# Chunk 0's first channel product in seven block products, batch 1's v loaded whole, two small transfers taken out

## The chip, the core and the metric

The kernel runs on one core of a Trainium2 chip, in one launch. Time is in microseconds (us) of that core, and lower is better. The core has five engines that run side by side and wait for each other by semaphores: TensorE (PE in the profile, its weight loads PEld) does matmuls, VectorE (DVE), ScalarE (ACT) and GpSimd (POOL) work element by element, and SyncE (SP) issues the DMA transfers. Each engine takes its own instructions strictly in order: one that waits holds back all behind it.

## The reference

Three layers follow each other. Inputs are float32; the batch is 2, the sequence 768, the model width 512.

```python
# 1: attention, 8 heads of 64: near scores in a window of 16, far scores on block maxima of k
k_sum = k.reshape(B, H, nb, 32, D).max(axis=3)
v_sum = v.reshape(B, H, nb, 32, D).mean(axis=3)
a = softmax([scores near, scores on k_sum + log(32)])
x = a @ concat([v, v_sum])
# 2: mixer
h = relu(x^T @ w_tok1) @ w_tok2            # 768 -> 256 -> 768, over tokens
u = x + h^T
y = u + relu(u @ w_ch1) @ w_ch2            # 512 -> 1536 -> 512, over channels
# 3: second mixer, xk and xr mix a token with the one before it
k = relu(xk @ w_k); v = (k * k) @ w_v      # 512 -> 1024 -> 512
out = sigmoid(xr @ w_r) * v
```

## The kernel before

**Precision.** A float32 product is made of three matmuls (`mm3`, L189 to L192): each operand is split into a rounded part ("high") and the rest ("low"), and high·high, high·low and low·high are summed in PSUM. Splitting costs one ScalarE operation (high) and one VectorE operation (low) for each tile of 128x512. Weights come as packed words; `conv_base` (`ca`) and `conv_top` (`cn`) on ScalarE and `conv_join` (`cj`, L428 and L429) on VectorE unpack a raw tile in place, then `conv_high` (`ch`) and `conv_low` (`cl`) split it. `conv_join` has the extra instruction L428 only for a tile for which `conv_top` was not called.

**Tiling.** Attention goes by 12 query tiles, 0 to 5 of batch 0 and 6 to 11 of batch 1: `scores` (`sc`), `softmax` (`max`: a VectorE maximum over 704 columns and a subtraction), `exp_near`/`exp_far` (`en`, `ef`), transposes (`tr`, copied out by `tc`), `pv` (the product with v) and `xnorm` (`norm`). Each tile is then split (`xh`, `xl`) and goes through `tok1` (`t1`); `tok2` (`t2`) makes u = x + h^T for a channel tile of 128 and leaves it in PSUM. The channel mixer goes by three chunks of 512 tokens: chunk 0 is batch 0 only, chunk 1 holds the end of batch 0 and the start of batch 1, chunk 2 the rest.

**Two ways to make u @ w_ch1.** Chunk 0 does it plainly: `tok2_high` (L553) and `tok2_low` (L557) split u, `ch1` (L563) runs 12 output tiles of 12 matmuls 128x512, and `ch1_high`/`ch1_low` make relu and its split. Chunks 1 and 2 use seven block products in place of eight (the scheme of Strassen), for each of three groups d of 512 outputs: `x_sum` (`bs`), `x_high` (`bh`) and `x_low` (`bl`) form seven combinations of the inputs; `form_sum` (`ws`), `form_high` (`wh`) and `form_low` (`wl`) seven combinations of the weights (letter `e`), in part kept in HBM by `form_store` (`wst`) and read back by `form_load` (`wld`); `product` (`p`, L700) runs 12 matmuls 128x256 for each; `prod_copy` (`pc`, ScalarE) and seven `prod_add` (`pa`, L727, VectorE) add the products up from PSUM; `h2_high` and `h2_low` (`gh`, `gl`) make relu and its split. For the forms of chunks 1 and 2 eight raw tiles are read a second time (`ld e`). `ch2` (`c2`) multiplies by w_ch2 into an accumulator, and `y_high` (`yh`) adds u. The second mixer also uses seven products throughout.

**Buffers.** One pool of 48 SBUF tiles serves nearly everything. In PSUM there are two single banks (`psum`) and three pairs. The next `psum` waits until its bank has been read.

**Order.** The order of the whole program is a string, `PLAN` (from L44), of some 1,700 short operations. A loop at the end (L840) calls the function of each name; so every engine's queue has the order of `PLAN`. All DMAs go on SP's queue. A `gate` (L199; `gk`, `gq`, `gv`, `gb`, `gw`, `gx`, `gu`) is a transfer of 4 bytes of a tile into `gate_sb`: since SP waits with it until the tile has landed, it holds back the transfers behind it in the queue. `gw c 0 0` and `gw c 1 0` do this with the raw weight tiles `rawc_0` of rows 0 and 1. Since `conv_join` writes the raw tile in place, it must wait until the gate has read it:

```python
def gate(t):
    ...
    load(gate_sb[:, n:n + 1], t[0:1])
```

**v.** A query tile's v is a tile of four planes. `load_v` loads two of them (260 KB; three for the last tile of a batch), and `overlap` (`vu`, L246 to L249) on GpSimd copies the others from these and from the next tile.

Of the kernel before, what the change touches and what calls it, by code (L numbers as in the profile page):

```python
# [50 lines left out]
cj t1 2,mu,pv 3,ld t2 2,xl 2,norm 3,ch t1 2,t1 1,t1 2,xh 3,xl 3,gw t2 1,cl t1 2,lk 1 0,lk 1 1,ca t2 0,cn t2 0,pv 4,norm 4
cj t2 0,gw t2 2,ca t2 2,lk 1 2,xh 4,pv 5,xl 4,ch t2 0,norm 5,br,lq 1 0,ca t2 1,cn t2 1,cl t2 0,cj t2 1,t1 3,lk 1 3,lv 6,t1 4
xh 5,xl 5,gk 1 2,km 1 2,t1 5,gq 1 0,t2x 0 0 0,cn t2 2,cj t2 2,ch t2 1,ld c 0 0,lq 1 1,gk 1 3,om,cl t2 1,gq 0 2,lb 0 1,t1h 0 0
t1l 0 0,ld c 1 0,gv 6,t2x 0 1 0,ch t2 2,lb 0 0,gq 1 1,t1h 0 1,cl t2 2,gk 1 1,km 1 1,t1l 0 1,t2 0 0 0,km 1 0,km 1 3,t2 0 1 0
# [5 lines left out]
tc 8 0,tc 8 1,en 10,tr 9 0,pad 11,max 11,ef 10,pv 7,tr 9 1,tc 9 0,xh 6,t2 0 3 1,tc 9 1,en 11,xl 6,ef 11,norm 7,c1 0 0  # L60
t2h 0 3 1,xh 7,xl 7,tr 10 0,pv 8,c1h 0 0,tc 10 0,c1l 0 0,c1 0 1,norm 8,xh 8,xl 8,tr 10 1,tc 10 1,c1h 0 1,pv 9,tr 11 0,pv 10
tc 11 0,c1l 0 1,norm 9,tr 11 1,t1 6,norm 10,xh 9,tc 11 1,pv 11,xl 9,t1 7,xh 10,norm 11,ld c 0 1,ca c 0 1,xl 10,ld c 2 0
ld c 3 0,ld c 2 1,ld c 3 1,ca c 3 0,gu 0 3 1,ld c 1 1,gx 10,gx 8,ld c 4 0,ld c 5 0,ld c 7 0,ca c 2 0,cn c 0 1,cj c 0 1
ch c 0 1,ld c 6 1,cl c 0 1,gx 9,ld c 4 1,ld c 6 0,ld c 11 0,ld c 5 1,t1 8,t1 9,cn c 3 0,ld c 8 0,cn c 2 0,cj c 2 0,ca c 1 1
# [863 lines left out]
```

## Time and profile before

| | |
|---|---|
| time, median of 3 runs (lowest to highest) | 457.39 us (457.03 to 457.98) |
| profiled execution, its own time | 459.92 us |
| its span, first to last instruction | 458.1 us |
| mean granted clock of TensorE | 0.996 |
| TensorE busy | 444.0 us (97%) |
| VectorE busy | 365.6 us (80%) |
| ScalarE busy | 278.7 us (61%) |
| GpSimd busy | 39.1 us (9%) |

The profile is of one execution, whose own time is 1.8 us above its span and 2.5 us above the median. Matmuls are pipelined, so that a matmul's duration is longer than its distance to the next; the distance is what it costs. TensorE is busy nearly throughout; the gaps are in the first 70 us and at the very end.

### The profile page before, as it was taken

How to read it: one execution, taken by the hardware profiler on the slowest of the kernel's cores; microseconds unless marked ns; L12 is line 12 of the kernel's file. 1: busy time of each engine (PE TensorE's matmuls, PEld its weight loads, DVE VectorE, ACT ScalarE, POOL GpSimd, SP SyncE). 2: the span in 40 equal slices, each digit the busy share in tenths (PEclk: the TensorE clock that was granted, in tenths of full speed). 3: DMA queues.
4: the chain of work that ended last, by engine and by line, in shares of the span. 5: the costliest groups of instructions: out<-in, count | busy, mean ns of one | idle time of the engine just before them, and what ended most of it. 6: DMA issues, size and time to landing. Idle time of an engine off the chain costs nothing.

```text
span 458.1 us, 10628 instructions
## 1 busy us (share of the span) xinstructions
PE 444.0 (97%) x4264; PEld 388.8 (85%) x4264; DVE 365.6 (80%) x580; ACT 278.7 (61%) x504; POOL 39.1 (9%) x110
## 2 busy tenths in 40 slices
PE   7999699999999999999999999999999999999996
PEld 4677578878888889989898988888989999999995
DVE  4678798467788548989968729998899989999865
ACT  1497337479987443386644427987887763864530
POOL 1760185000000000000000000000000000000000
PEclk9999989999999999999999999999999999999999
DMA  7768852569555400770696894893979994984902
GB/s 278 230 183 286 302 168 82 200 236 395 242 185 181 187 0 1 273 278 2 219 397 257 308 411 201 318 389 121 357 254 387 355 392 148 355 287 153 344 1 92
DMA packets 33925, 108.31 MB, mean 236 GB/s; under 512 B 3797, under 2 KB 7381, under 8 KB 33877
## 3 DMA queue, kind: packets, MB, share of 16 engines
q1 hardware_dynamic: 33876, 107.65, 64.7%
q8 instruction: 33, 0.54, 0.5%
q14 instruction: 16, 0.12, 0.1%
HBM read 80.89 MB, written 26.74 MB: 235 GB/s over the span
## 4 chain that ended last, share of the span: by engine, by line
PE 83%; DMA 8%; SPq 3%; DVE 2%; POOL 2%; issue 1%; DVEq 0%; POOLq 0%
PE p L190 9%; PE p L192 8%; PE p L191 8%; PE acc L190 7%; PE acc L191 7%; PE acc L192 7%; PE v L192 4%; PE v L190 4%; PE v L191 4%; SPq L195 3%; DMA rawt<-in_w 3%; PE r L190 2%; PE h L190 2%; PE h L192 2%; PE h L191 2%; PE r L192 2%
## 5 line engine op out<-in xcount | busy, mean ns | idle before, releaser
L727 DVE TENSOR_TENSOR ev<-p,ev 128x512 f32<-128x512 f32 x84 | 56.4, 687 | 19.0 <-PE p L192 16.4
L190 PE MATMUL p<-xs,wba 128*128 128x256 f32 x168 | 47.4, 282 | 0.0
L192 PE MATMUL v<-wbv,k 128*128 128x256 f32 x168 | 47.1, 280 | 0.0
L192 PE MATMUL p<-xs,wba 128*128 128x256 f32 x168 | 47.1, 280 | 0.0
L191 PE MATMUL v<-wbv,k 128*128 128x256 f32 x168 | 47.1, 280 | 0.0
L190 PE MATMUL v<-wbv,k 128*128 128x256 f32 x168 | 47.1, 280 | 0.0
L191 PE MATMUL p<-xs,wba 128*128 128x256 f32 x168 | 47.1, 280 | 0.0
L190 PE MATMUL acc<-hq,wc 128*128 128x512 f32 x96 | 37.9, 395 | 0.0
L191 PE MATMUL acc<-hq,wc 128*128 128x512 f32 x96 | 37.8, 394 | 0.0
L192 PE MATMUL acc<-hq,wc 128*128 128x512 f32 x96 | 37.7, 393 | 0.0
L597 ACT ACTIVATE hq<-ev 128x512 fp32r<-128x512 f32 x24 | 14.9, 631 | 32.6 <-DVE ev L727 27.2
L190 PEld LDWEIGHTS p<-xs,wba 128*128 128x128 f32 x168 | 31.7, 188 | 0.3 <-DVE ev L727 0.2
L191 PEld LDWEIGHTS p<-xs,wba 128*128 128x128 f32 x168 | 31.7, 188 | 0.1
L190 PEld LDWEIGHTS v<-wbv,k 128*128 128x128 f32 x168 | 31.7, 189 | 0.0
L191 PEld LDWEIGHTS v<-wbv,k 128*128 128x128 f32 x168 | 31.7, 188 | 0.0
L192 PEld LDWEIGHTS v<-wbv,k 128*128 128x128 f32 x168 | 31.7, 189 | 0.0
L192 PEld LDWEIGHTS p<-xs,wba 128*128 128x128 f32 x168 | 31.7, 188 | 0.0
L190 PE MATMUL p<-xs,wae 128*128 128x256 f32 x88 | 24.7, 281 | 0.0
L191 PE MATMUL p<-xs,wae 128*128 128x256 f32 x88 | 24.6, 280 | 0.0
L192 PE MATMUL p<-xs,wae 128*128 128x256 f32 x88 | 24.6, 280 | 0.0
L720 ACT COPY ev<-p 128x512 f32<-128x512 f32 x12 | 7.0, 586 | 27.0 <-PE p L192 27.0
L532 PE MATMUL u<-wt,h 128*128 128x256 f32 (+1 forms) x120 | 21.7, 322 | 1.2 <-DVE wt L436 0.6
(174 smaller groups left out, 1306.2 us busy)
## 6 DMA issues: line engine op xcount, KB each, us to landing
wba<-kepta SPq DMA_DIRECT2D x28, 512.0 KB
wbv<-keptv SPq DMA_DIRECT2D x28, 512.0 KB
rawc<-in_wc SPq DMA_DIRECT2D x24, 512.0 KB
kepta<-waa SPq DMA_DIRECT2D x14, 512.0 KB
wbe<-kepte SPq DMA_DIRECT2D x14, 512.0 KB
keptv<-wav SPq DMA_DIRECT2D x14, 512.0 KB
rawe<-in_wc SPq DMA_DIRECT2D x8, 512.0 KB
...
```

The lines of the kernel that those rows point to most:

```text
L190: PE.matmul(o, lhsT=wh, rhs=xh, start=start, stop=False)
L191: PE.matmul(o, lhsT=wh, rhs=xl, start=False, stop=False)
L192: PE.matmul(o, lhsT=wl, rhs=xh, start=False, stop=stop)
L195: nc.sync.dma_start(out=out, in_=in_)
L532: PE.matmul(ps[:, dst:dst + m], lhsT=h1[b, k][:, low, d], rhs=x[:, i, o:o + m], start=False, stop=low == 1 and k == 1 and pi == len(pieces ...
L597: A.activation(out=h2_block(c, d, q, 0), in_=x, func=AF.Relu)
L720: A.copy(out=block(z, c, d, 0), in_=pr[z, c, d, 0])
L727: V.tensor_tensor(out=block(z, c, d, o), in0=pr[z, c, d, p], in1=block(z, c, d, x), op=ALU.add)
```

## The change

It has four parts, and with them nearly the whole of `PLAN` from its 100th operation on is written in another order.

1. Chunk 0's u @ w_ch1 is made by the seven block products too. Its 21 products all use the two single banks. `ch1`, `ch1_high`, `ch1_low`, `tok2_low` and `y_low` are gone; `tok2_high` writes u unsplit into y.
2. The weight combinations `e` are formed once, from the raw tiles `c`, before chunk 0, all 21 of them are stored, and each later use loads them (`wld e` 14 before, 28 after; `wst e` 14 before, 21 after). The eight second reads `ld e` and their `ca`, `cn` and `cj` are gone, as are 12 `ch` and 12 `cl` of w_ch1.
3. `load_v` loads all four planes for batch 1 (520 KB a tile) from an input `vo` arranged so; `overlap` of batch 1's six tiles is gone.
4. `gw c 0 0` and `gw c 1 0` are gone.

Counted over the program, `p` goes from 42 to 63 in the channel mixer, `pa` likewise, and VectorE has 11 instruction rows more, ScalarE 12 fewer.

```diff
 PLAN (two lines of it)
-t2 0 2 0,gw c 0 0,t2h 0 0 0,t2l 0 0 0,lb 1 1,t2 0 3 0,lb 1 0,gw c 1 0,ca c 0 0,cj c 0 0,pad 6,t2h 0 1 0,t2l 0 1 0,bq 0 0,lv 7
+lb 1 0,pad 7,ld c 2 0,t2 0 3 0,gb 0 0,t2h 0 1 0,bh 0 0 0,lb 1 1,bl 0 0 0,gq 0 2,gb 0 1,ca c 0 0,cj c 0 0,ca c 1 0,km 1 3
...
     def load_v(u):
         vw[u] = slot([P, 4, NP * VW], f"vw{u}")
-        load(vw[u][:, 0:2, :], vp[u, :, 0:2])
-        if u % QT == QT - 1:
-            load(vw[u][:, VJ[3], :], vp[u, :, 2])
+        if u < QT:
+            load(vw[u][:, 0:2, :], vp[u, :, 0:2])
+            if u == QT - 1:
+                load(vw[u][:, VJ[3], :], vp[u, :, 2])
+        else:
+            load(vw[u], vo[u - QT])
...
     def form_raw(z, d, j, w):
-        key = ("c", 4 * d + j, 0) if z == "e" and d == 2 else (z, d, j)
-        return words(cv[key], F32)[w]
+        return words(cv[("c", 4 * d + j, 0) if z == "e" else (z, d, j)], F32)[w]
...
     def tok2_high(b, dt, g):
         dst, ps = upart(b, dt, g)
-        A.copy(out=dst if W2[b][g][0] else dst[:, 0], in_=ps)
-
-    def tok2_low(*a):
-        dst, ps = upart(*a)
-        V.tensor_tensor(out=dst[:, 1], in0=ps, in1=dst[:, 0], op=ALU.subtract)
+        A.copy(out=dst, in_=ps)
...
-    def ch1(c, f):
-        ps = psum(f"h2_{c}_{f}")
...
     def y_high(c, k):
-        V.tensor_tensor(out=yk(c, k)[:, 1:CH + 1], in0=acc[c, k // 2][:, k % 2, :], in1=yk(c, k)[:, 1:CH + 1] if c else uc[c, k][:, 0], op=ALU.add)
-
-    def y_low(c, k):
...
+        V.tensor_tensor(out=yk(c, k)[:, 1:CH + 1], in0=acc[c, k // 2][:, k % 2, :], in1=yk(c, k)[:, 1:CH + 1], op=ALU.add)
...
+    WHICH = {(0, 0): (), (0, 1): (), (0, 2): (), (1, 2): (), (1, 1): (1,), (1, 0): (1,), (2, 0): (1,), (2, 1): (2,), (2, 2): (2,)}
+
     def product(z, c, d, p):
-        if z:
+        if z or c == 0:
             pr[z, c, d, p] = psum(f"p{z}{c}_{d}_{p}")
...
-        w, x = wa["a", d, p, TURN[c, d]] if z else form("e", d, p), xs[z, c, p]
+        w, x = wa["a", d, p, TURN[c, d]] if z else wa[("e", d, p) + WHICH[c, d]], xs[z, c, p]
```

**Where the order moves.** On VectorE around the first `conv_join` of w_ch1, before the change (`uc` is chunk 0's split u, `rawc` a raw tile of w_ch1, `kp` a tile of k, `vsb` block sums of v, `mx` and `e` a query tile's maxima and scores, L557 `tok2_low`):

```order
L253 TENSOR_REDUCE kp_0_759<-kp_0_759 128x24
L253 TENSOR_REDUCE kp_3_872<-kp_3_872 128x24
L557 TENSOR_TENSOR uc_0_980<-u_0_0_895,uc_0_980 128x512
L428 TENSOR_SCALAR rawc_0_904<-rawc_0_904 128x512
L429 SCALAR_TENSOR_TENSOR rawc_0_904<-rawc_0_904 128x512
L557 TENSOR_TENSOR uc_1_1010<-u_1_0_920,uc_1_1010 128x512
L269 TENSOR_REDUCE vsb<-vb_927 128x32
L428 TENSOR_SCALAR rawc_0_917<-rawc_0_917 128x512
L429 SCALAR_TENSOR_TENSOR rawc_0_917<-rawc_0_917 128x512
L269 TENSOR_REDUCE vsb<-vb_912 128x32
L557 TENSOR_TENSOR uc_3_1025<-u_3_0_985,uc_3_1025 128x512
L436 TENSOR_TENSOR wc_0_1111<-rawc_0_904,wc_0_1111 128x512
L330 TENSOR_REDUCE mx<-sc_1027 128x8
L332 TENSOR_TENSOR e_1158<-sc_1027,mx 128x704
```

The same place after the change (`xs` is a combination of inputs, L642 `x_low`; `wae` a combination of weights, L466 `form_low`; L258 `kmax`):

```order
L258 TENSOR_REDUCE kp_2_634<-kp_2_634 128x24
L258 TENSOR_REDUCE kp_0_763<-kp_0_763 128x24
L642 TENSOR_TENSOR xs_0_987<-y_0_959,xs_0_987 128x512
L432 TENSOR_SCALAR rawc_0_909<-rawc_0_909 128x512
L433 SCALAR_TENSOR_TENSOR rawc_0_909<-rawc_0_909 128x512
L258 TENSOR_REDUCE kp_3_864<-kp_3_864 128x24
L432 TENSOR_SCALAR rawc_0_924<-rawc_0_924 128x512
L433 SCALAR_TENSOR_TENSOR rawc_0_924<-rawc_0_924 128x512
L466 TENSOR_TENSOR wae_0_1002<-rawc_0_909,wae_0_1002 128x512
L335 TENSOR_REDUCE mx<-sc_1036 128x8
L337 TENSOR_TENSOR e_1090<-sc_1036,mx 128x704
```

The two `tok2_low` that stood around the first in-place write of `rawc` are gone, and the maximum of a k tile now stands behind it.

On VectorE some 50 instructions later, before the change (L429 `conv_join`, L436 `conv_low`, L488 the split of `tok1`'s or chunk 0's relu, L396 `xl`):

```order
L429 SCALAR_TENSOR_TENSOR rawc_0_1774<-rawc_0_1774 128x512
L488 SCALAR_TENSOR_TENSOR h_0_2_1874<-h_0_2_1843,h_0_2_1874 128x512
L429 SCALAR_TENSOR_TENSOR rawc_0_1776<-rawc_0_1776 128x512
L436 TENSOR_TENSOR wc_1_1861<-rawc_1_1764,wc_1_1861 128x512
L436 TENSOR_TENSOR wc_0_1888<-rawc_0_1774,wc_0_1888 128x512
L436 TENSOR_TENSOR wc_0_1896<-rawc_0_1776,wc_0_1896 128x512
L429 SCALAR_TENSOR_TENSOR rawc_1_1766<-rawc_1_1766 128x512
L396 TENSOR_TENSOR xhl_1919<-xf_2_1700,xhl_1919 128x512
L436 TENSOR_TENSOR wc_1_1924<-rawc_1_1766,wc_1_1924 128x512
```

The corresponding part after the change, just ahead of the first `ch2` (`ev` is a sum of block products, L696 `prod_add`; L458 `form_sum`; `hq` the split relu, L573; the last row is the split of the weights that the first `ch2` reads):

```order
L696 TENSOR_TENSOR ev_1_1_2006<-p_1_1_1971,ev_1_0_1952 128x512
L466 TENSOR_TENSOR wae_6_2010<-rawc_0_1795,wae_6_2010 128x512
L458 TENSOR_TENSOR rawc_0_1769<-rawc_0_1769,rawc_0_1771 128x512
L466 TENSOR_TENSOR wae_3_1966<-rawc_0_1795,wae_3_1966 128x512
L696 TENSOR_TENSOR ev_1_0_1952<-p_1_5_1990,ev_1_0_1952 128x512
L466 TENSOR_TENSOR wae_4_1984<-rawc_0_1792,wae_4_1984 128x512
L696 TENSOR_TENSOR ev_1_0_1952<-p_1_6_2026,ev_1_0_1952 128x512
L466 TENSOR_TENSOR wae_2_2018<-rawc_0_1769,wae_2_2018 128x512
L573 SCALAR_TENSOR_TENSOR hq_101_2057<-ev_1_1_2006,hq_100_2053 128x2x256
L696 TENSOR_TENSOR ev_1_0_1952<-p_1_4_2040,ev_1_0_1952 128x512
L696 TENSOR_TENSOR ev_1_1_2006<-p_1_4_2040,ev_1_0_1952 128x512
L696 TENSOR_TENSOR ev_1_0_1952<-p_1_2_2060,ev_1_0_1952 128x512
L440 TENSOR_TENSOR wc_1_1933<-rawc_1_1789,wc_1_1933 128x512
```

Where weights were converted one after the other, sums of products out of PSUM now alternate with weight combinations. In the queue after the change there are 93 rows from the first maximum of batch 1 (`mx<-sc_1036`) to that last row: 6 `max` (12 rows), 4 block sums of v (L274), 6 `norm` (12 rows), 2 L432, and 63 others of 128x512 elements: 13 `form_low`, 13 `prod_add`, 8 `form_sum`, 7 L433 of `conv_join`, 6 `xl`, 6 `x_low`, 4 `x_sum`, 5 `h2_low` and 1 `conv_low`. TensorE in the same stretch, up to the first `ch2`, has 14 block products, and beside them exactly the work that it has before the change up to the end of the last `tok1`, without that time's 6 `ch1` output tiles and 18 `ch2`.

## Rows read from the trace of the kernel before

**Rows 1.** The page: the span and the share of TensorE.

```profile
span 458.1 us, 10628 instructions
...
PE 444.0 (97%) x4264; PEld 388.8 (85%) x4264; DVE 365.6 (80%) x580; ACT 278.7 (61%) x504; POOL 39.1 (9%) x110
```

**Rows 2.** Waits of TensorE over the whole span, then from 68 to 454 us (us, times, longest).

```profile
PE u L518 <- DVE uc L557: 3.2, 2, 2.8
...
PE et L358 <- POOL vw L249: 0.4, 1, 0.4
PE p L190 <- DVE ev L727: 0.2, 1, 0.2
```

**Rows 3.** Timeline of TensorE, 52 to 64 us: start, duration, instruction, idle before.

```profile
53.41 1.65 PE L532 MATMUL u<-wt,h 128*128 128x256 f32 x12
57.88 0.66 PE L518 MATMUL u<-cst,xf 128*128 128x128 f32 x4 [2.82 <-DVE uc L557]
58.30 2.23 PE L532 MATMUL u<-wt,h 128*128 128x256 f32 x12
60.46 1.96 PE L319 MATMUL sc<-kp,q 64*32 64x128 f32 x64
...
62.63 1.16 PE L319 MATMUL sc<-kp,q 64*32 64x128 f32 x64
```

**Rows 4.** By stretch: busy us of PE, PEld, DVE, ACT, POOL; clock; DMA; GB/s.

```profile
57.00:62.00 5.00, 4.12 (x80) 3.85 (x80) 4.90 (x7) 1.38 (x3) 3.21 (x7) 0.71 0.78 263
...
60.00:120.00 60.00, 59.56 (x1038) 47.79 (x1038) 42.81 (x66) 43.52 (x86) 14.95 (x35) 0.98 0.64 228
```

**Rows 5.** The chain that ended last, 44 to 72 us: start, us, what.

```profile
50.31 5.60 DMA gate_sb<-rawc
```

**Rows 6.** Timeline of ScalarE, 48 to 53 us.

```profile
51.77 0.68 ACT L416 ACTIVATE rawc<-rawc 128x512 f32<-128x512 f32 x1
```

**Rows 7.** Timeline of VectorE, 48 to 73 us.

```profile
52.28 0.67 DVE L557 TENSOR_TENSOR uc<-u,uc 128x512 fp32r<-128x512 f32 x1
56.00 0.43 DVE L428 TENSOR_SCALAR rawc<-rawc 128x512 uint32<-128x512 uint32 x1 [3.06 <-DMA gate_sb<-rawc]
...
67.68 2.34 DVE L269 TENSOR_REDUCE vsb<-vb 128x32 f32<-128x1024 f32 x2
69.94 0.88 DVE L330 TENSOR_REDUCE mx<-sc 128x8 f32<-128x704 f32 x1
...
71.66 0.88 DVE L330 TENSOR_REDUCE mx<-sc 128x8 f32<-128x704 f32 x1
```

**Rows 8.** Timeline of VectorE, later: a normalisation, then three equal operations in a row.

```profile
89.87 0.20 DVE L386 RECIPROCAL dn<-xo 128x8 f32<-128x8 f32 x1
90.10 0.69 DVE L387 TENSOR_TENSOR xf<-xo,dn 128x512 f32<-128x512 f32 x1
...
221.60 1.89 DVE L470 TENSOR_TENSOR waa<-rawa,waa 128x512 fp32r<-128x512 f32 x3
```

**Rows 9.** Timeline of TensorE: chunk 0's matmuls, tok1's last, a block product's.

```profile
80.29 0.39 PE L190 MATMUL h<-uc,wc 128*128 128x512 f32 x1
...
82.85 0.40 PE L192 MATMUL h<-uc,wc 128*128 128x512 f32 x1
...
125.31 0.39 PE L192 MATMUL t<-xhl,wt 128*128 128x512 f32 x1
...
174.18 0.28 PE L190 MATMUL p<-xs,wc 128*128 128x256 f32 x1
...
182.58 0.28 PE L192 MATMUL p<-xs,wae 128*128 128x256 f32 x1
```

**Rows 10.** What VectorE waited for from 60 to 180 us (us, times, longest).

```profile
DVE h L488 <- ACT h L485: 7.3, 5, 3.0
...
DVE rawc L429 <- ACT rawc L423: 5.5, 7, 1.8
```

**Rows 11.** The page: the DMA queue, packets, MB, share of 16 engines.

```profile
q1 hardware_dynamic: 33876, 107.65, 64.7%
```

More of the change, by code (lines that the diff above doesn't have):

```diff
@@ L51 @@
[L51 to L54, printed above, removed]
@@ L60 @@
[L60 to L64, printed above, removed]
@@ new lines @@
+tr 8 0,norm 6,ws e 0 0,tr 8 1,ye 0 1,sc 11,max 11,ws e 0 1,tc 8 0,en 10,ef 10,tr 9 0,tc 8 1,tr 9 1,tc 9 0,tc 9 1,xh 6
+t2 0 3 1,t2h 0 3 1,en 11,xl 6,pv 7,ef 11,norm 7,bs 0 0 2,bs 0 0 1,wh e 0 5,p 0 0 0 0,pc 0 0 0,xh 7,xl 7,tr 10 0,wl e 0 5
+tc 10 0,tr 10 1,pv 8,norm 8,tc 10 1,ws e 0 2,bs 0 0 3,bh 0 0 5,bh 0 0 6,xh 8,xl 8,ws e 0 3,bl 0 0 5,pv 10,tr 11 0,tc 11 0
+p 0 0 0 1,pa 0 0 0 0,pv 9,bh 0 0 4,norm 9,bl 0 0 4,norm 10,wh e 0 6,tr 11 1,tc 11 1,t1 6,wst e 0 0,xh 9,bl 0 0 6,wl e 0 6
+pv 11,wh e 0 4,wl e 0 4,t1 7,xl 9,xh 10,norm 11,xl 10,ld c 2 1,gu 0 3 1,gh 0 0 0,ld c 4 1,wst e 0 1,ld c 5 0,ld c 4 0
@@ new lines @@
+c2 2 11 1,ma 1 1 3,wst v 0 5,mh 1 1 1,c2 2 11 2,wld a 0 1 0,yh 2 0,mh 1 1 2,mh 1 1 3,c2 2 11 3,yh 2 2,yh 2 3,mp 0 0 3
+wld a 0 5 0,yh 2 1,mp 2 1 0,mp 0 0 0,r 0 0,ml 1 1 0,wld a 0 6 0,ml 1 1 1,ml 1 1 2,wld a 0 3 0,r 0 1,rs 0 0,ml 1 1 3
+wld a 0 4 0,mp 2 1 1,mp 0 0 1,ma 0 0 0,mp 2 1 2,ma 0 0 1,mp 0 0 2,ma 0 0 3,bh 1 0 0,r 0 2,ma 0 0 2,rs 0 1,mp 2 1 3
+wld a 0 2 0,bl 1 0 0,bh 1 0 1,bs 1 0 0,bh 1 0 2,bl 1 0 1,bh 1 0 4,r 0 3,bs 1 0 1,rs 0 2,bs 1 0 2,bh 1 0 5,bl 1 0 5,bl 1 0 4
+bh 1 0 6,r 1 0,rs 0 3,wld a 1 0 0,ma 2 1 0,ma 2 1 1,mh 2 1 0,ld v 1 0,ma 2 1 2,mh 2 1 1,ma 2 1 3,r 1 1,mh 2 1 2,bl 1 0 2
@@ L603, in ch2 @@
     def ch2(c, f, dt):
-        h = (h2[c, f][:, 0, :], h2[c, f][:, 1, :]) if c == 0 else [hq[c, f // 4, f % 4 // 2, i][:, f % 2, :] for i in range(2)]
+        h = [hq[c, f // 4, f % 4 // 2, i][:, f % 2, :] for i in range(2)]
         w = wt["c", f, 1]
@@ L831, in block_kernel @@
             "ld": fetch, "ca": conv_base, "cn": conv_top, "cj": conv_join, "ch": conv_high, "cl": conv_low,
-            "t1": tok1, "t1h": tok1_high, "t1l": tok1_low, "t2": tok2, "t2x": tok2_x, "t2h": tok2_high, "t2l": tok2_low,
-            "c1": ch1, "c1h": ch1_high, "c1l": ch1_low, "c2": ch2, "ye": y_edge, "yh": y_high, "yl": y_low,
+            "t1": tok1, "t1h": tok1_high, "t1l": tok1_low, "t2": tok2, "t2x": tok2_x, "t2h": tok2_high,
+            "c2": ch2, "ye": y_edge, "yh": y_high,
             "mp": mix_prev, "ma": mix_add, "mh": mix_high, "ml": mix_low, "r": rgate, "rs": rsig,
@@ L918 @@
     maps, args = {}, []
-    for name in ("qT", "kT", "vp", "vb", "w1", "w2", "wc", "wk", "wv", "wr", "mu", "mask", "const"):
+    for name in ("qT", "kT", "vp", "vo", "vb", "w1", "w2", "wc", "wk", "wv", "wr", "mu", "mask", "const"):
         a = arrays[name]
```

266 lines of the change are left out of this document (122 added, 144 removed).

## The prediction

> **What bounds the kernel now.** I start with the busy shares: TensorE works 444.0 of 458.1 us [rows 1]. So the time is TensorE's own work plus some 14 us of gaps, and a change counts only by the work it takes from TensorE or the waits it takes away or makes there. The list of TensorE's waits shows where the gaps are: 3.2 us in two waits of u's transposes for `tok2_low`, and from 68 to 454 us only two waits of 0.4 and 0.2 us, of which one is for a sum of block products [rows 2]. TensorE is dense from 68 us on. There, less work is less time, as long as the engines that feed it keep up. VectorE had room to: from 60 to 120 us it worked 42.81 of 60 us, while TensorE worked 59.56 [rows 4].
>
> The gap stands at 53 to 62 us. The timeline shows a wait of 2.82 us ahead of the transposes at 57.88; the 12 matmuls of `tok2` behind it took 2.23 us where the same 12 took 1.65 before it; and 64 score matmuls took 1.96 where the next 64 took 1.16 [rows 3]. The granted clock from 57 to 62 us was 0.71 of full speed, TensorE having stood idle just before [rows 4]. The chain of waits names the cause: the 4-byte gate on `rawc`, issued at 50.31, landed 5.60 us later [rows 5]. The raw tile itself was there: ScalarE's `conv_base` was working on it at 51.77 [rows 6]. VectorE was through with `tok2_low` at 52.28 + 0.67 = 52.95, and then stood 3.06 us, since it must not write the tile before the gate has read it [rows 7]. The next `tok2_low` was queued behind that, and TensorE waited for its bank.
>
> **1. Fewer columns on TensorE.** 144 matmuls 128x512 go. Twelve starts in a row, 80.29 to 82.85, lie (82.85 − 80.29)/11 = 0.233 us apart: 33.5 us. 252 matmuls 128x256 (21 products of 12) come: from 174.18 to 182.58 are 71 distances of 0.118, so 1.42 us a product and 29.8 in all [rows 9]. TensorE saves 3.7 us. `tok2`, the scores and `ch2` stay as they are.
>
> **2. The stall goes.** Both gates on raw weights and the `tok2_low` around them are taken out. The waits of 3.2 us and the slow matmuls' 0.58 + 0.80 us are worth 4.6 us [rows 2, 3]. What is late next is the maximum of the last k tile, which in the new order stands behind the first `conv_join` on VectorE; I count it just in time, and if not, about 0.9 us comes back. So the scores of tile 6, which end just ahead of 62.63 in the old order, end at 62.6 − 4.6 = 58.0, and VectorE's maxima of batch 1 start there.
>
> The Trainium skill would price the gate lower: "DMA: Bandwidth & Descriptors", section "Latency and other measured facts", gives 0.6 us to the first byte and up to 2 us for HBM at high load, so that the gate would land at 52.9 by estimate, before VectorE came for the tile. By that rule part 2 would be worth nothing and the sum would come out 4.6 us higher. The measured 5.60 us decides against it [rows 5].
>
> **3. VectorE, from 58 us to the first `ch2`.** Here the head start meets a new bound. With 21 products in two banks, a product can start only once the sum before last has left its bank; and the last VectorE row ahead of the first `ch2` is the split of the weights that it reads. VectorE's queue from the first maximum of batch 1 to that row, as counted in the section on the change, takes:
> - 6 `max`, one every 71.66 − 69.94 = 1.72 us [rows 7]: 10.3;
> - 4 block sums, two in 2.34 [rows 7], less the 0.09 by which an operation's end overlaps the next one: 1.13 each, 4.5;
> - 6 `norm`, 90.10 − 89.87 = 0.23 for the reciprocal and 0.60 behind it [rows 8]: 5.0;
> - 63 other operations 128x512. Three in a row took 1.89, of which the last has 0.69, so one every 0.60 [rows 8]: 37.8;
> - 2 shifts L428 of 0.43 and their hand-over [rows 7]: 1.0.
>
> That is 58.6 us without a wait, and I add 1 us for waits: the first `ch2` at 58.0 + 59.6 = 117.6. TensorE's own side: before, the last `tok1` ended with its last matmul's start and one distance, at 125.31 + 0.23 = 125.54 [rows 9], by which time 6 `ch1` tiles (72 × 0.233 = 16.8) and 18 `ch2` (54 × 0.233 = 12.6) were done too, so all else took until 96.2. After, this same work and 14 products (19.9) would be done at 96.2 − 4.6 + 19.9 = 111.5. VectorE is some 6 us later than that. So TensorE waits some 6 us in this stretch, in small pieces, and what was gained in part 2 is spent: 117.6 − 19.9 = 97.7 against 96.2, a loss of 1.5 us. The bounds of this term: −4.6, if VectorE is not what ends last, and +6, if five hand-overs from ScalarE cost what such waits cost before, 12.8 us in 12 waits or 1.07 each [rows 10], in place of the 1 us that I add (1.5 − 1 + 5.4). I take +1.5, since VectorE's rows are counted and their durations measured, and what is estimated is only the 1 us.
>
> **4. Behind the first `ch2`.** The first `ch2` stands behind the first two groups of seven products. From there on `ch2` groups of 3 × 0.233 = 0.7 us, which need no sum from VectorE, stand between the products of the third, and VectorE loses 12 splits of relu, 12 `conv_low`, 8 `conv_join` and 4 `y_low`. Up to chunk 1 I count VectorE's rows at less than TensorE's, so TensorE is dense again. Some first waits for `h2_low` and weights are left: between 0.2 (the one that such a sum cost before [rows 2]) and 1.6 us; I take 0.9. Chunks 1 and 2 and the second mixer are the same work in nearly the same order; 0.
>
> **5. Transfers and GpSimd.** 14 more `wld e` and 7 more `wst e` of 512 KB come, 8 `ld e` go, and v of batch 1 is 12 half tiles of 260 KB where there were some 6.5. That is some 8.3 MB beside 107.65 [rows 11]. At the rate of the trace, 64.7% of 458.1 us for 107.65 MB, it is 23 us of the queue, spread over 200. I cost it at nothing: the 16 engines are free a third of the time, and each load stands at least 6 us of TensorE's work ahead of its use. GpSimd's copies of v, which cost TensorE 0.4 us [rows 2], go for batch 1; that is within the estimate of part 4.
>
> **Sum.** −3.7 + 1.5 + 0.9 = −1.3 us; part 2's 4.6 us is contained in the second term. The profiled execution took 459.92 with a span of 458.1 [rows 1]; so 458.6. The median is 457.39, and what changes is a count of work and waits that both have: 457.39 − 1.3 = 456.1 us. Likely between 454.4 and 457.6, for 1.7 us either way in terms 3 and 4.
>
> **Rivals.** A. *VectorE does not bind:* its 58.6 us start earlier than I put them, since part of the 63 operations need nothing of batch 1's scores and some wait only in my count. For it: they were movable, and VectorE had a third of its time free. Against: their place in the queue is fixed, and the maxima at its head wait for the scores. Then part 2 is gained in part or in full: −3.7 − 4.6 + 0.9 = −7.4 at most, 450.0; half of it, 453. Chance 0.14.
>
> B. *VectorE waits for ScalarE (slower).* 31 of the 63 operations (`form_low`, `x_low`, `xl`, `h2_low`, `conv_low`) need the rounded half from ScalarE just before. Where VectorE is the bound every such wait is TensorE's too. Before, such waits were 1.07 us each [rows 10] and cost nothing. Four of them beyond the 1 us counted give +4.3: 460.4. It decides from +2.2 us on, two waits. Chance 0.18.
>
> C. *The clock falls in the waits.* TensorE would stand still for 6 us in pieces. The one time that it stood 2.82 us, the clock cost 0.58 + 0.80 = 1.4 us behind it [rows 3, 4]. Against: the pieces are below 1 us, and after the waits of 0.2 and 0.4 us nothing is seen [rows 2]. One or two such falls: 457.5 to 458.9. Chance 0.09. The Trainium skill has this as a rule ("TensorE: Matmul & The Clock Gate", section "A second HAM failure mode: psum-queue depth-cycling"): matmul groups that cycle through PSUM banks with micro-idles in between make the clock swing between its levels. Before the change no row shows it.
>
> D. *A transfer is late.* Without the gates the loads behind them start earlier and share the engines with v's 520 KB, so that the first raw tile lands late and a wait like the old one returns, from 1 us to the whole 4.6: 457.1 to 460.7. For it: the DMA share was 0.78 at 57 to 62 us [rows 4]. Against: `conv_base` had the tile by 51.77 even behind the gates [rows 6]. Chance 0.09. The page's rule in part 2 gives this rival's upper end, 460.7: the wait would never have been the gate's.
>
> **How the numbers follow.** A measurement can tell 0.2%, about 0.9 us, from no change: faster is below 456.5, slower above 458.3. The forecast has 0.50 (0.37 faster, 0.13 same); A 0.14, all faster; B 0.18, all slower; C 0.09 (0.06 same, 0.03 slower); D 0.09 (0.05 same, 0.04 slower). Faster 0.51, same 0.24, slower 0.25. The range goes from 452.0, which leaves out the far half of A, to 460.5, which takes in most of B and all of C and D.
>
> **What would show it.** In the changed kernel's profile: no wait for a gate near 55 us, and the clock at full there; the scores of tile 6 done near 58; VectorE busy for nearly all of 58 to 117 us and TensorE waiting for `prod_add` and weight splits in it; the first `ch2` at 117 to 118; TensorE dense from 125 us on; TensorE's busy time some 3 to 4 us less. I am wrong if the first `ch2` comes before 114 (A) or after 120 (B), if the granted clock drops between 60 and 117 (C), or if a wait for a transfer of over 1 us stands on TensorE's or VectorE's list (D).

## The result, and the profile after

The changed kernel takes 462.63 us (median of 4 runs, 459.16 to 465.73), the kernel before beside it 457.21: a ratio of 1.0121, 95% interval 1.0081 to 1.0162. It is slower by about 1.2%, where 456.1 and a range up to 460.5 were predicted. The profiled execution took 464.34 us; its page has the span, TensorE's busy time and the DMA queue [rows 1, 11]:

```profile
span 462.6 us, 10816 instructions
...
PE 443.7 (96%) x4372; PEld 393.3 (85%) x4372; DVE 371.6 (80%) x592; ACT 270.8 (59%) x490; POOL 21.9 (5%) x76
...
q1 hardware_dynamic: 35600, 115.93, 69.1%
```

TensorE is busy as long as before, not 3 to 4 us less, and in a longer span. Its waits over the whole span [rows 2] have new names at their head:

```profile
PE sc L324 <- issue: 4.0, 3, 3.3
PE et L363 <- issue: 2.3, 1, 2.3
...
PE p L194 <- DVE wae L466: 0.3, 1, 0.3
```

"issue" means that TensorE waited for nothing that the profile names. The wait for `tok2_low` is gone, and waits for sums or weights are 0.3 us at most: in the waits that this list shows, VectorE hardly holds TensorE up where the prediction looked for it. Before, there was nothing of the kind from 68 us on [rows 2]. TensorE's timeline has the two long standstills, and the first `ch2` (`acc`) [rows 3, 9]:

```profile
76.25 0.91 PE L324 MATMUL sc<-kp,q 64*32 64x128 f32 x45 [3.26 <-issue]
...
93.82 0.38 PE L363 MATMUL et<-cst,e 128*128 128x128 f32 x2 [2.28 <-issue]
...
124.87 0.40 PE L192 MATMUL acc<-hq,wc 128*128 128x512 f32 x1
```

By stretch (columns as in [rows 4]): the clock is full at 57 to 62 us, where it was 0.71; it falls twice, to 0.63 at 78 to 82 us and to 0.58 at 94 to 98, behind the two long standstills; and VectorE works 52.82 of the 60 us that follow 60, TensorE 51.52, where it was 59.56:

```profile
57.00:62.00 5.00, 4.88 (x104) 3.92 (x92) 4.89 (x7) 2.38 (x5) 0.22 (x3) 1.00 0.98 324
60.00:120.00 60.00, 51.52 (x926) 42.87 (x924) 52.82 (x84) 40.34 (x81) 0.00 (x0) 0.94 0.70 239
78.00:82.00 4.00, 3.70 (x65) 2.95 (x67) 2.40 (x4) 2.44 (x6) 0.00 (x0) 0.63 0.00 0
94.00:98.00 4.00, 4.00 (x60) 2.82 (x63) 2.50 (x5) 3.77 (x8) 0.00 (x0) 0.58 1.09 387
```

VectorE's timeline, from the first maximum of batch 1 to the split that the first `ch2` reads [rows 7, 8]:

```profile
58.10 0.88 DVE L335 TENSOR_REDUCE mx<-sc 128x8 f32<-128x704 f32 x1
...
82.44 0.21 DVE L391 RECIPROCAL dn<-xo 128x8 f32<-128x8 f32 x1 [2.00 <-PE xo L381]
...
98.50 0.21 DVE L391 RECIPROCAL dn<-xo 128x8 f32<-128x8 f32 x1 [1.49 <-PE xo L381]
...
101.50 0.69 DVE L696 TENSOR_TENSOR ev<-p,ev 128x512 f32<-128x512 f32 x1 [0.86 <-PE p L194]
...
123.77 0.68 DVE L440 TENSOR_TENSOR wc<-rawc,wc 128x512 fp32r<-128x512 f32 x1
```

Its waits in this stretch, 58 to 124 us, come to 6.6 us, of which 5.3 are for TensorE and 1.3 for ScalarE [rows 10]:

```profile
DVE dn L391 <- PE xo L381: 3.9, 3, 2.0
DVE ev L696 <- PE p L194: 0.9, 1, 0.9
DVE xhl L401 <- ACT xhl L397: 0.8, 1, 0.8
DVE wae L466 <- ACT wae L463: 0.5, 1, 0.5
DVE mx L335 <- PE sc L330: 0.5, 1, 0.5
```

VectorE waits for TensorE's `pv` (`xo`) until 82.4 and 98.5, 6.2 and 4.7 us after TensorE goes on from standstills that VectorE had no part in. What it waits is not made up, since its queue is full.

**What TensorE stood still for.** Counting matmuls and weight loads up to each `issue` wait (the two counts of a row added) gives 2475, 2729, 2983 and 3749:

```profile
0.00:63.11 63.11, 57.74 (x1237) 42.59 (x1238) 45.02 (x67) 34.53 (x68) 20.15 (x64) 1.00 0.82 275
0.00:68.74 68.74, 62.16 (x1364) 45.56 (x1365) 50.58 (x73) 38.10 (x77) 20.15 (x64) 1.00 0.77 257
0.00:73.00 73.00, 66.02 (x1491) 48.37 (x1492) 54.67 (x79) 41.25 (x85) 20.15 (x64) 1.00 0.78 257
0.00:91.50 91.50, 80.67 (x1874) 60.67 (x1875) 69.33 (x103) 51.78 (x106) 20.15 (x64) 0.98 0.73 241
```

The distances are 254, 254 and 766 = 3 × 255.3: every standstill is at one and the same place in a grid of about 256 instructions. With the few other records of TensorE's queue that these views leave out, the trace counts 2497, 2753, 3009 and 3777 up to the four: 256, 256 and 3 × 256 apart. Of two DMA queues named "instruction", the page shows one with packets of 16 KB (packets, MB, share):

```profile
q8 instruction: 34, 0.56, 0.5%
```

34 packets for 4372 matmuls and 4372 weight loads is one packet for 257 of TensorE's instructions. Around the longest standstill, 72.99 to 76.25, the DMA queues show no such packet from 67.6 to 73.8 us, while data takes 85% of the engines, and one from 73.8 to 74.8:

```profile
q1 hardware_dynamic: 417, 1.56, 85.4%
...
q8 instruction: 1, 0.02, 5.5%
```

In the trace's packet records this one runs from 73.84 to 74.72, and TensorE goes on 1.53 us after its end. That is so in every case: of all 16 traces here together, 33 of TensorE's `issue` waits stand at such an edge, and each ends 1.3 to 1.5 us after the end of a 16-KB packet (four others, of 0.4 us, in the kernel before and its variants, stand elsewhere). The packet also tells what was late. Ahead of the two long standstills it came 4.8 and 4.0 us after TensorE had passed the edge before, and TensorE needs only some 4 us for a block here (69.01 to 72.99). At 76.25, with little data on the way, it came after 1.0.

What filled the queue is in SP's timeline: two v loads of 520 KB and a store of `wae` just before it, and six raw weights in a row ahead of the standstill of 91.5:

```profile
68.11 0.81 SPq L197 DMA_DIRECT2D vw<-in_vo  x2
68.97 0.42 SPq L197 DMA_DIRECT2D kepte<-wae  x1
...
85.26 6.63 SPq L197 DMA_DIRECT2D rawc<-in_wc  x6
```

So TensorE's next block of instructions queues behind bursts of data, and TensorE stands still at the block's edge. What is left to test is what moves these standstills and what they cost. The Trainium skill ("Runtime: NRT & Kernel Launch", section "Instruction fetch mechanics") has the block of 256 instructions, fetched by DMA, and calls the cost of crossing an edge "mostly hidden". The spacing agrees; the cost, 3.26 and 2.28 us here, does not.

### The profile page after: what moved, and what is told of

It is laid out like the page before. It is cut to its first block, busy times and chain, and to the rows that moved or that the text cites. A ratio compares the mean times of both kernels' runs of the same rounds, so it can differ in the third digit from the quotient of the medians.

```text
span 462.6 us, 10816 instructions
## 1 busy us (share of the span) xinstructions
PE 443.7 (96%) x4372; PEld 393.3 (85%) x4372; DVE 371.6 (80%) x592; ACT 270.8 (59%) x490; POOL 21.9 (5%) x76
## 3 DMA queue, kind: packets, MB, share of 16 engines
q1 hardware_dynamic: 35600, 115.93, 69.1%
## 4 chain that ended last, share of the span: by engine, by line
PE 83%; DVE 6%; DMA 3%; issue 3%; ACT 2%; SPq 2%; DVEq 0%; ACTq 0%
PE p L192 10%; PE p L194 10%; PE p L193 10%; PE acc L192 7%; PE acc L194 7%; PE acc L193 7%; PE v L193 4%; PE v L194 4%; PE v L192 4%; PE u L528 3%; DMA q<-in_qT 2%; PE r L192 2%; PE r L194 2%; PE r L193 2%; PE xo L381 2%
## 5 line engine op out<-in xcount | busy, mean ns | idle before, releaser
L696 DVE TENSOR_TENSOR ev<-p,ev 128x512 f32<-128x512 f32 x105 | 70.2, 686 | 31.7 <-PE p L194 26.6
L192 PE MATMUL acc<-hq,wc 128*128 128x512 f32 x144 | 56.7, 394 | 0.0
L194 PE MATMUL acc<-hq,wc 128*128 128x512 f32 x144 | 56.7, 393 | 0.0
L193 PE MATMUL acc<-hq,wc 128*128 128x512 f32 x144 | 56.6, 393 | 0.0
L569 ACT ACTIVATE hq<-ev 128x512 fp32r<-128x512 f32 x36 | 22.3, 632 | 41.8 <-DVE ev L696 33.5
L192 PE MATMUL p<-xs,wbe 128*128 128x256 f32 x140 | 39.2, 280 | 0.0
L194 PE MATMUL p<-xs,wbe 128*128 128x256 f32 x140 | 39.2, 280 | 0.0
L193 PE MATMUL p<-xs,wbe 128*128 128x256 f32 x140 | 39.2, 280 | 0.0
L689 ACT COPY ev<-p 128x512 f32<-128x512 f32 x15 | 8.8, 589 | 48.0 <-PE p L194 47.8
L192 PE MATMUL p<-xs,wae 128*128 128x256 f32 x112 | 32.1, 287 | 0.6 <-DVE ev L696 0.3
L194 PEld LDWEIGHTS acc<-hq,wc 128*128 128x128 f32 x144 | 27.0, 188 | 6.6 <-DVE wc L440 0.4
L194 PE MATMUL p<-xs,wae 128*128 128x256 f32 x112 | 31.7, 283 | 0.4 <-DVE wae L466 0.3
L192 PEld LDWEIGHTS p<-xs,wba 128*128 128x128 f32 x168 | 31.7, 189 | 0.2
L193 PEld LDWEIGHTS acc<-hq,wc 128*128 128x128 f32 x144 | 27.1, 188 | 5.7
L192 PEld LDWEIGHTS acc<-hq,wc 128*128 128x128 f32 x144 | 27.1, 188 | 5.6
L192 PEld LDWEIGHTS v<-wbv,k 128*128 128x128 f32 x168 | 31.8, 189 | 0.0
```

Of the source, the lines that this page charges most:

```text
L192: PE.matmul(o, lhsT=wh, rhs=xh, start=start, stop=False)
L193: PE.matmul(o, lhsT=wh, rhs=xl, start=False, stop=False)
L194: PE.matmul(o, lhsT=wl, rhs=xh, start=False, stop=stop)
L569: A.activation(out=h2_block(c, d, q, 0), in_=x, func=AF.Relu)
L689: A.copy(out=block(z, c, d, 0), in_=pr[z, c, d, 0])
L696: V.tensor_tensor(out=block(z, c, d, o), in0=pr[z, c, d, p], in1=block(z, c, d, x), op=ALU.add)
```

## The experiments

Each kernel is compared with the kernel before on the same chip. In ten profiled executions of the changed kernel and its variants but one (`c2` moved forward) the time less the start of the first `ch2` is 339.0 to 340.1 us, mean 339.6 (464.34 − 124.87 in the one above). So the first `ch2` tells the time of an execution, and it must come at 457.2 − 339.6 = 117.6 for no change.

**1. Each kernel once more, unchanged.** One more execution of each, to see which stalls belong to the kernel and which to one execution.

> The kernel before once more, for a second profile. The profiled execution took 459.92 us, the median of 35 others 456.8, and the kernel without the two gates takes the same 456.7. Theory S (the long stall on the gate was a matter of that one execution): the gate on rawc lands 1 to 3 us sooner than the 5.60 us, the wait for tok2_low is below 2 us, and the time is 456 to 458. If the stall is the rule: a wait of 2.5 to 3.5 us again at a time near 457, and then the gain of taking the gates out is lost elsewhere.

> The changed kernel once more, for a second profile. Theory F: standstills of TensorE without a releaser at the same counts of its instructions (near 167 modulo 256), of other lengths than 3.26 and 2.28 us, since what stands in the queue at that moment varies; the time goes with their sum: below 2 us in sum about 460, above 5 us 464 or more. Theory V: VectorE's queue from the first maximum to the first conv_low takes 62 to 66 us again.

Before took 456.71. VectorE's wait for the gate, from its timeline, and the gate in the chain of waits:

```profile
54.42 0.43 DVE L428 TENSOR_SCALAR rawc<-rawc 128x512 uint32<-128x512 uint32 x1 [0.96 <-DMA gate_sb<-rawc]
...
51.12 3.20 DMA gate_sb<-rawc
```

The gate landed after 3.20 us, not 5.60; VectorE stood 0.96 us, not 3.06; TensorE's waits for `tok2_low` were 1.1 in all, not 3.2. The profiled execution on which part 2 rested, 2.5 us above the median, held a stall of which the second execution has a third. After took 464.31: standstills of 0.36, 0.42, 2.18 and 2.04 us, first `ch2` at 124.74, VectorE's waits 5.8. The standstills are the kernel's own; their sizes vary, and so does the edge that has the long one: at the edge of the 3.26 us the second execution stood 0.42, and 2.18 at the next one.

**2. Parts 4 and 3 on the kernel before.**

```diff
-t2 0 2 0,gw c 0 0,t2h 0 0 0,...,lb 1 0,gw c 1 0,ca c 0 0
+t2 0 2 0,t2h 0 0 0,...,lb 1 0,ca c 0 0
```

> Kernel before, with the two gates on raw weights taken out and nothing else (part 4 alone). Theory G (the 4.6 us of the stall at 53 to 62 us are the gate's, and TensorE is dense behind it): no wait of over 0.5 us for tok2_low, and 3 to 4.6 us faster than before, 452.5 to 454. Rival L (the load itself, or VectorE's queue, is late next): the wait shrinks to 1 to 2 us, and 1 to 2 us are gained. Rival F (TensorE's instruction blocks): the transfers that the gates held back start earlier and standstills without a releaser of 1 to 3 us stand between 60 and 95 us, so that 0 to 2 us are gained.

The other takes `overlap` of batch 1 (`vu 6` to `vu 11`) out and loads v whole:

> Kernel before, with batch 1's v loaded whole and GpSimd's six overlaps of it left out (part 3 alone). Theory F: 1.5 MB more of transfers between 53 and 75 us, standstills of TensorE without a releaser of up to 2 us there; the wait of 0.4 us for GpSimd's copies goes: -0.4 to +2 us. Theory V, and the prediction's part 5: between -0.5 and 0 us, no standstill.

> Kernel before with parts 3 and 4 together, and chunk 0 still by plain products. Theory G: as the one without gates, 3 to 4.6 us faster than before, since TensorE remains dense. Theory F: at least 1.5 us slower than the one without gates alone.

Without the two gates 456.74 (0.9977, 0.9949 to 1.0004); v whole 457.76 (0.9999, 0.9963 to 1.0035); both 457.62 (0.9986, 0.9953 to 1.0018). Neither part moves the time of before by more than can be measured, so the forecast gain of 3 to 4.6 us without the gates is missed. TensorE's waits for `tok2_low` are 3.2, 1.1 and 2.1 us in the three profiles with the gates, 0.7 and 1.6 in the two without: part 2's 4.6 us are not there to be had. Nor do the standstills need the block products: with v whole, and with both, TensorE stood still at one of the same edges (count 2729), in the kernel before:

```profile
PE sc L322 <- issue: 0.9, 1, 0.9
PE sc L322 <- issue: 2.3, 1, 2.3
```

The second of these two executions took 460.27, against its kernel's median of 457.62; the medians do not show it. The loss comes with the block products and the new order, or with their meeting the rest; part 1 was not tried alone.

**3. v as halves in the changed kernel** (part 3 undone).

```diff
-            load(vw[u], vo[u - QT])
+            load(vw[u][:, 0:2, :], vo[u - QT][:, 0:2])
+            if u % QT == QT - 1:
+                load(vw[u][:, VJ[3], :], vo[u - QT][:, VJ[3]])
 PLAN: vu 6 to vu 11 put back, on GpSimd
```

> Changed kernel with part 3 undone: v of batch 1 loaded as halves of 260 KB and completed by copies on GpSimd, in otherwise the same order. Theory F: the transfers ahead of the instruction block at 73 us are half as long, the standstill there falls from 3.26 to about 1 to 2 us, and the kernel is 1 to 3 us faster than the changed one. Theory V: the same time, or up to 0.5 us slower for waits on GpSimd's copies.

460.96 (1.0096, 1.0076 to 1.0117). TensorE's standstills:

```profile
74.98 0.91 PE L326 MATMUL sc<-kp,q 64*32 64x128 f32 x45 [1.10 <-issue]
...
91.52 0.38 PE L365 MATMUL et<-cst,e 128*128 128x128 f32 x2 [2.20 <-issue]
```

The one at the v loads is 1.10 in place of 3.26, the one at the raw weights, which were left as they are, stays. Since the sizes vary between two executions of the changed kernel too, one profile of each shows little about what the halves did. The first `ch2` comes at 121.18, 3.7 us earlier than in the changed kernel's profile; the medians are 1.7 us apart, less than the spread of the changed kernel's runs. VectorE's waits from 58 to 121 us are now all but gone:

```profile
DVE ev L698 <- PE p L194: 0.9, 1, 0.9
DVE wae L468 <- ACT wae L465: 0.2, 1, 0.2
```

It runs from 59.02 to the split at 120.11 + 0.60: 61.7 us with 1.1 of waits, so 60.6 of work where 58.6 was counted; GpSimd's copies are back beside it here. That is a bound of its own: with hardly a wait the first `ch2` of this kernel does not come before 120.

**4. The v loads paced** by gates on the tile before (`gv 9`, `gv 10`, `gv 11`), so that they do not come in a burst.

```diff
-t2 0 2 1,lv 10,t2 0 1 1,t2h 0 0 1,t2h 0 1 1,lv 11,sc 8,ef 6
+t2 0 2 1,gv 9,lv 10,t2 0 1 1,t2h 0 0 1,t2h 0 1 1,gv 10,lv 11,gv 11,sc 8,ef 6
```

> Changed kernel, with three more 4-byte gates that let v of query tiles 9, 10 and 11 and the first stored weight form go one after the other instead of together. Theory F (fetch): TensorE stood still 3.26 us at 73 us, amid score matmuls that wait for nothing, because its next block of instructions (16 KB by the DMA queue q8) came behind these four transfers of 512 KB; then the block gets through, that standstill is below 1.5 us, and the kernel is 2 to 4 us faster than the changed one. Theory V (VectorE alone sets the stretch up to the first ch2, by hand-overs from ScalarE): no change beyond 0.7 us.

461.23 (1.0091, 1.0067 to 1.0115), first `ch2` at 122.91. TensorE's waits:

```profile
PE p L192 <- ACT rawc L427: 2.4, 1, 2.4
...
PE xo L381 <- issue: 0.9, 1, 0.9
```

The one standstill left, 0.9 us, is at 36 to 37 us; from 58 us to the first `ch2` there is none, with the same work and, but for the three gates, the same bytes. For the v loads that speaks for the burst. But the raw tiles still came six in a row, from 90.28 us, and no standstill followed: the packet was 6.0 us behind the edge before it, and TensorE took 10.2 us over that block. So a burst costs time only where TensorE runs through a block faster than the packet comes. What was gained went mostly into a new wait of 2.4 us for a raw tile, whose load stands behind the gates on SP's queue: 1.4 us by the medians, for 2 to 4 forecast, and within the two intervals.

**5. The grid moved.** 32 tiny matmuls take the place of one matmul of the warm-up at the start, so that every later instruction stands 31 matmuls and 31 weight loads further on in its block.

```diff
-heat 6,lq 0 1,sc 0
+heat 5,tiny 32,lq 0 1,sc 0
```

> Changed kernel with 32 tiny matmuls (8 columns) at the very start in place of one of the six warm-up products, so that every later TensorE instruction stands some 60 instructions further back in its 256-instruction block. Theory F: the standstills without a releaser stay, but in front of other instructions, some 30 matmuls earlier in the program (not at the 20th score matmul of query tile 11), at the same count of TensorE instructions modulo 256 as before; their lengths may be others, time within 3 us of the changed kernel. If a hidden wait of that score matmul were the cause, it would stand still at the same matmul as before.

464.83 (1.0173, 1.0129 to 1.0218). The standstills, and the counts up to them:

```profile
72.39 0.30 PE L386 MATMUL xo<-vw,et 64*32 64x65 f32 x2 [0.19 <-issue]
80.67 0.57 PE L386 MATMUL xo<-vw,et 64*32 64x65 f32 x35 [1.32 <-issue]
92.08 0.46 PE L386 MATMUL xo<-vw,et 64*32 64x65 f32 x30 [2.05 <-issue]
```

```profile
0.00:72.20 72.20, 64.38 (x1492) 48.32 (x1492) 52.62 (x76) 39.76 (x81) 20.07 (x64) 0.98 0.76 250
0.00:79.30 79.30, 70.36 (x1619) 52.66 (x1619) 59.48 (x87) 45.16 (x93) 20.07 (x64) 0.98 0.76 248
0.00:90.00 90.00, 79.45 (x1874) 60.42 (x1875) 69.28 (x103) 51.86 (x106) 20.07 (x64) 0.98 0.74 241
```

They stand at 2984, 3238 and 3749, the counts of the kernel unshifted (2983, its neighbour 254 on, 3749), but at other matmuls: `xo` in place of `sc` and `et`. So they belong to the instruction count and not to a matmul or its operands.

**6. More data.** Three transfers of 512 KB within HBM behind the last v load.

```diff
-lv 11,sc 8,ef 6
+lv 11,xd 0,xd 1,xd 2,sc 8,ef 6
```

> Changed kernel with three more transfers of 512 KB, from HBM to HBM, right behind the load of v of query tile 11, which nothing waits for. Theory F: the instruction block that TensorE waits for at 73 us comes 3 to 5 us later still, so that the standstill there grows from 3.3 to 6 to 8 us, and the kernel takes 2 to 4 us more. If transfers had no part in the standstills: no change beyond 1 us.

A miss: 459.44 in its one execution, first `ch2` at 120.47, standstills of 0.34 us at 69.1 and 1.20 at 85.1. The `gv` gates landed some 4 us later in this execution, so that v's loads were issued at 71.3 to 75.4, in place of 67.0 to 69.0. The amount of data alone does not make the standstill; what fits is when it is issued against the block. A dose was not shown.

**7. VectorE relieved.** First by GpSimd, which takes the eight `form_sum` of the first two groups (`G` in place of `V`):

```diff
-        V.tensor_tensor(out=form_raw(z, d, dst, 1), ...
+        (G if z == "e" and d < 2 else V).tensor_tensor(out=form_raw(z, d, dst, 1), ...
```

> Changed kernel with the 8 form_sum of weight groups 0 and 1 moved from VectorE to GpSimd, which has nothing else to do there; VectorE has 8 x 0.60 = 4.8 us less up to the first ch2. Theory V: the first ch2 comes 4 to 5 us earlier than at 124.9 and the kernel is as much faster. Theory F: TensorE's standstills remain (3 to 6 us in sum), VectorE binds only behind the last of them, so 0 to 3 us are gained.

465.07 (1.0171, 1.0146 to 1.0196), first `ch2` at 126.11. GpSimd's timeline, and VectorE's beside it:

```profile
77.45 5.39 POOL L458 TENSOR_TENSOR rawc<-rawc,rawc 128x512 f32<-128x512 f32 x3
...
78.25 1.26 DVE L401 TENSOR_TENSOR xhl<-xf,xhl 128x512 fp32r<-128x512 f32 x1
...
81.37 2.02 DVE L629 TENSOR_TENSOR xt<-y,xt 128x512 f32<-128x512 f32 x1
```

GpSimd needs 5.39 / 3 = 1.8 us for a sum, and VectorE's operations beside it take 1.26 and 2.02 in place of 0.68. From the first maximum to the split VectorE works 62.0 us with eight operations fewer, for 59.8 in the changed kernel: the relief costs more than it frees, and both forecasts of a gain are missed. The standstills are there too, 2.98 us for the longest. Then, on the kernel with half v, the eight `form_sum` left out altogether (that part of the weight combinations is not computed):

```diff
-ws e 0 0,  -ws e 0 1,  -ws e 0 2,  -ws e 0 3,  -ws e 1 0,  -ws e 1 1,  -ws e 1 2,  -ws e 1 3
```

> The changed kernel with v in halves, and the 8 form_sum of weight groups 0 and 1 left out (the combinations of weights are then not those of the product; all else runs as it did). VectorE has 8 x 0.60 = 4.8 us less to do up to the first ch2. If VectorE's queue sets that stretch even where TensorE hardly stands still: first ch2 at 116.5 to 117.5 in place of 121.2 and 4 to 4.8 us faster than with the sums. If TensorE's standstills set it: less than 1.5 us faster.

459.85 (1.0037, 1.0002 to 1.0072), first `ch2` at 120.26. 4.8 us of VectorE's work gone bring 0.9 there and 1.1 in the median; VectorE's waits rise from 1.1 to 5.6 us. TensorE, with its standstill of 2.3 us and a clock of 0.72 at 88 to 94 us, where the kernel with half v kept the full clock, is as long.

**8. The raw loads paced** on the kernel with half v, then also without the `form_sum` (left out as in 7).

```diff
-ld c 4 1,wst e 0 1,ld c 5 0,ld c 4 0
+ld c 4 1,gx 8,wst e 0 1,ld c 5 0,gx 9,ld c 4 0
```

> Half_v with two more gates on transfers already asked for, put between the six raw loads that SP issues together at 85 us, so that the instruction block that TensorE asks for near 90 us is not behind them. Theory (TensorE's blocks queue behind bursts of transfers, and VectorE's queue by itself is as long): the 2.2 us standstill near 91 shrinks below 1 us; but VectorE has hardly a free us up to the first ch2 in half_v (60.1 us of work in 61.1), so the first ch2 comes at 120 to 121 as there and the time is 0 to 1 us below half_v's 460.96. Rival 1 (the standstill alone decides): first ch2 at 118 to 119, 2 us faster than half_v. Rival 2 (bursts of loads have nothing to do with it): the standstill near 91 stays above 2 us.

> The same kernel without the eight form_sum of the first two weight groups on VectorE (left out of the computation). Theory (two bounds of about equal length, VectorE's queue and TensorE with its standstills): with both relieved the first ch2 comes at 116 to 118 and the time is 3 to 4 us below half_v's, where leaving out the form_sum alone gave 1.1 us and the pacing alone 0 to 1. Rival 1 (a third wait, for ScalarE, takes their place): the first ch2 stays at 119 to 121, and VectorE's waits in 58 to 120 us are for ScalarE's results. Rival 2 (the standstill moves to another burst of loads): a new standstill of over 1 us before 115.

461.65 (1.0103, 1.008 to 1.0125) and 460.02 (1.0068, 1.0042 to 1.0094), first `ch2` at 122.52 and 121.20. In both the standstill near 91 us is gone: in the first kernel the block's packet came 0.8 us after the edge before it, in place of 4.0 in half v. The one at the v loads, which were not paced here, is gone as well in this execution. The first has no `issue` wait at all from 58 us to its first `ch2`, the second two, of 0.63 and 1.46 us, ahead of 72. But the loads now land late. ScalarE's timeline of the second kernel, and VectorE's waits from 58 to 124 us:

```profile
100.86 0.67 ACT L422 ACTIVATE rawc<-rawc 128x512 f32<-128x512 f32 x1 [2.83 <-DMA rawc<-in_wc]
```

```profile
DVE wae L468 <- ACT wae L465: 2.5, 2, 1.6
DVE dn L393 <- PE xo L383: 1.0, 2, 0.7
DVE xs L644 <- ACT xs L641: 1.0, 1, 1.0
```

So the forecast for the standstill near 91 held, and both for the first `ch2` were missed: the first kernel's came at 122.52 for 120 to 121, with the time of half v within the intervals, and the second's 3 to 4 us are not there: rival 1, a third wait, took the place (4.1 of VectorE's 5.5 us are for ScalarE). From 85 to 100 us either TensorE's block or the raw tiles are late.

**9. `ch2` moved forward**, the first eight between the products of the second group (on half v).

```diff
-p 0 0 1 0 / pc 0 0 1,... p 0 0 1 1,wh e 1 4,...
+p 0 0 1 0,c2 0 0 0,c2 0 0 1 / pc 0 0 1,... p 0 0 1 1,c2 0 0 2,c2 0 0 3,wh e 1 4,...
```

> Changed kernel with v in halves, and the first 8 ch2 (5.6 us of TensorE, for which VectorE has only 4 operations or 2.4 us to do) moved ahead, in between the second group's block products, where TensorE waits for VectorE. Theory V: TensorE works in 3 to 5 us of its waits, and the kernel is 2 to 4 us faster than with v in halves alone: 457 to 459. Theory F: the waits at that place are not VectorE's, and less than 1 us is gained.

466.35 (1.0221, 1.0169 to 1.0272). That is 5.4 us above half v, where neither forecast had a loss. The waits moved and grew; TensorE's from 100 to 135 us:

```profile
PE acc L192 <- ACT wc L439: 4.2, 1, 4.2
```

VectorE waited 3.7 us for products meanwhile. No version tried beats the kernel before by more than can be measured.

## Why the prediction was wrong

**Part 1** (−3.7 us of columns) is not contradicted: a product that nothing held up took 1.42 us (111.26 to 112.68 on TensorE's timeline), as counted, and behind the first `ch2` TensorE has no wait above 0.3 us, and the time left from there is 339.6 where the sum implied 458.6 − 117.6 = 341.0. That TensorE's busy time did not fall is no measure of it, since work at the lower clock counts as busy for longer. **Part 4**'s 0.9 us was not paid, which is most of these 1.4.

**Part 2** named a wait that exists. That the maxima began at 58.10 for 58.0 forecast is in part luck: in the second execution they began at 58.80, in the variants of the changed kernel at 57.7 to 59.8. The failed step is in the sum: "what changes is a count of work and waits that both have." The stall of 4.6 us was in the profiled execution and not in the median: experiment 1 shows 1.1 us of the 3.2 (2.1 in the kernel with v whole), and 64 scores in 1.16 us from the first on; experiment 2 shows that taking the gates out gains 0 to 0.5%. The place forecast for the first `ch2`, and with it 458.6, has no stall in it; taking 2.5 us more off for the median takes the stall off twice. The Trainium skill's price of a gate ("DMA: Bandwidth & Descriptors", section "Latency and other measured facts"), 0.6 us to the first byte and up to 2 us for HBM, an estimate of 2.6, is missed by the 3.20 too; but what it would make of part 2, nothing, is nearer to experiment 2 than the 4.6.

**Part 3** failed at "I add 1 us for waits". Of the 7.3 us by which the first `ch2` is late (124.87 for 117.6) 0.1 is the start, 1.2 VectorE's work (123.77 + 0.60 − 58.10 = 66.3, less 6.5 of waits before rounding, is 59.8, for 58.6), 5.5 the waits, and 0.5 the hand-over from the split. Rival B had the waits but put them to ScalarE, with 1.3 us of the 6.6. They came from TensorE, which the part had as 6 us ahead of VectorE: that lead was used up by 6.3 us of standstills and by the lower clock behind them, some 3.2 us by estimate (4.00 × 0.37 + 4.00 × 0.42, from the two rows of the clock). So in this execution TensorE, not VectorE, was the later one: 111.5 + 6.3 + 3.2 = 121.0 before any wait for another engine, against 58.10 + 59.8 + 0.5 = 118.4.

**Part 5** is where their cause lies: "I cost it at nothing: the 16 engines are free a third of the time". The mean was true, 69.1% for the whole, but the loads go in bursts, and what was queued behind them was not data that had time but TensorE's instructions. The packets show it directly; experiments 4 and 8 spaced the loads, and the standstills behind them went; experiment 5 moved the grid, and they moved with it; experiment 6 failed to show a dose. No rival had it: D looked for a late raw tile. **Rival C**'s clock fell (0.63 at 78 to 82 us, 0.58 at 94 to 98), each time after a long standstill, of 3.26 and 2.28 us, instead of many small waits; the kernel with half v stood 2.20 us with a mean clock of 1.000, so the fall does not follow each time. A slip without weight: 1.7 us above 456.1 is 457.8, not 457.6.

**The account.** By the relation above a median execution has its first `ch2` at 462.6 − 339.6 = 123.0: 5.4 us late. With 2.5 for the step to the median and −1.4 for the time behind it that is 6.5 = 462.6 − 456.1. How the 5.4 divide is only bounded. VectorE's queue by its own work makes 118.4 in the changed kernel, 0.8 late, and 120.1 in the kernel with half v, 2.5 late (with a start 0.9 us later and 0.8 us more of work, GpSimd's copies beside it). The rest, 2.9 to 4.6, is waits: the standstills, the clock behind them, and what VectorE waited for ScalarE. The parts do not add: leaving out 4.8 us of VectorE's work brought 1.1, and pacing the loads brought nothing.

**Open:** why the `gv` gates land up to 4 us earlier or later from one execution to the next, which moves the standstills and spreads the runs; how a standstill grows with the data ahead of the block (experiment 6); how much of the time the standstills alone cost, since no kernel without them was faster by more than can be measured; and whether an order exists in which VectorE, the blocks and the raw tiles are all in time.

## What to carry to other kernels

A stall that is taken from one profile is worth to the median what it is in a usual execution: where the profiled time lies well above the median, look at a second profile before the stall goes into a sum. Where an engine with hundreds of short instructions meets bursts of loads, its own instruction blocks are one more transfer that can be late, and a free mean share of the DMA engines says nothing of that. Its sign here was an engine that waits for nothing that the profile names, at steps of 256 of its own instructions. A new bound that is as long as the old one gives back what was saved, and three bounds of one length cannot be relieved one at a time.
